# Norm scales taken out of the weights, packed mean squares and reordered instruction lists in a fused Mamba-2 and SwiGLU kernel

## The chip, the cores and the metric

The kernel runs on one core of one Trainium2 chip. The metric is device time of that core in microseconds (us), the median of several executions. Before the change it was 423.63 us (three runs, 423.05 to 426.83).

The engines that matter are TensorE (PE in the profile; PEld is its weight load), VectorE (DVE), ScalarE (ACT) and GpSimd (POOL). Each runs its own queue of instructions; semaphores order them against one another.

## The reference, cut to what matters

```python
# x: 4 x 8 heads x 768 x 32, chunks of 32 tokens; all float32
for c in range(nc):                      # Mamba-2 (SSD), chunk by chunk
    y_intra = einsum(M, xc)              # M = (C B^T) * causal decay
    y_inter = einsum(Cc, state) * exp(cum)
    y[chunk] = y_intra + y_inter
    state = exp(sum(la)) * state + sum(Bx)
x = y as (3072 tokens, 256)
rms = sqrt(mean(x * x) + 1e-6)           # then the feed-forward block
xn  = x / rms * rms_g
out = (silu(xn @ w_gate) * (xn @ w_val)) @ w_out     # d_ff = 1536
```

## The kernel before

The 3072 tokens go in six blocks of 512. For each block the kernel makes y from the chunks (its own chunks are of 128 tokens, 24 in all, taken in 12 pairs), norms it, and multiplies by the gate, value and output weights. From block 1 on the products are done in Strassen's way: seven products (`P.1` to `P.7`) for eight, with sums and differences of the inputs (`tx`) and of the weights (`sw`, `two`). The stage before block 1's first such product is called the prologue here. In it the float32 weights are also built out of the raw 64-bit words that they arrive in.

The last instruction of that building multiplies mantissa by power of two. It also carries the norm's gain, which differs between the two halves `t` of the model dimension, so it is done twice for every gate or value piece:

```python
def weight(k):
    ...
    if is_o:
        nc.vector.scalar_tensor_tensor(out=dst, in0=f, scalar=2.0 ** -20, in1=e, ...)
    else:
        for t in range(2):
            nc.vector.scalar_tensor_tensor(out=dst[:, t], in0=f[:, t],
                                           scalar=g20[:, t:t + 1], in1=e[:, t], ...)
```

The norm takes eight matmuls with one column of 1/256, then the roots on GpSimd and a transpose that spreads them:

```python
def norm_sums(blk):                               # step "ms"
    ps["m"] = ms = bank("ms", (P, NT))
    for k in range(NT):
        nc.tensor.matmul(out=ms[:, k:k + 1], lhsT=sqs[blk][:, k * P:(k + 1) * P],
                         rhs=mean1, start=True, stop=True)
def norm_roots():                                 # step "rs"
    nc.vector.tensor_scalar_add(me, ps.pop("m"), 1e-6)
    nc.gpsimd.tensor_tensor(out=rs, in0=me, in1=nhalf, op=ALU.pow)
```

(The loop has four steps; the trace shows eight instructions a norm, since a float32 matmul is two.) The y products of a pair of chunks go in this order, which one of the experiments changes:

```python
if not first:
    inter(0, True)        # state product of chunk 0: 32-row, 64-column tiles
intra(0, first)           # products inside the chunks: 32-column tiles
intra(1, False)
inter(1, False)           # state product of chunk 1
```

What runs when is set by lists of steps. There is one list for the prologue with block 0, one for block 1, one for blocks 2 to 4 and one for block 5. All engines' instructions are issued in the list's order. A few steps of the steady list:

```text
... hid.21.1 P.6.3 table C.12.0 Tt.1.1.0 ... s.1 A.0 S.0 Tt.1.0.1 y.0 take.6.2 ...
... s4.0 O.5.5 ms O.6.3 s2.5 s4.2 O.2.2 ... O.7.0 rs s4.1 O.7.1 ... rb O.7.3 ... xn ... tx
```

`P.k.j` is a Strassen product, `take` ScalarE's copy of it, `C`, `silu`, `hid` what follows it, `O` an output product, `A`, `S`, `y` the state and y products of a pair, `ex` an exponential, and `table` loads SiLU's activation table. `rb` spreads the roots and `xn` multiplies by them.

## Time and profile before

| | before |
|---|---|
| time, median | 423.63 us |
| span of the profiled run (itself timed 422.98) | 421.3 us |
| block 1's first Strassen product | 101.5 us |
| blocks 1, 2, 3, 4 (first product to next block's first) | 64.9, 65.0, 65.6, 65.5 us |
| block 5 to the last product's start, then the tail | 54.9, 3.8 us |
| table loads | 17 |

The page of the profile before, busy times with shares of the span and instruction counts, and the shares of the chain that ended last:

```profile
PE 410.1 (97%) x3094; PEld 347.5 (82%) x3094; DVE 309.1 (73%) x669; ACT 226.5 (54%) x455; POOL 38.0 (9%) x48
...
PE 80%; DVE 13%; ACT 5%; issue 1%; DVEq 0%
```

TensorE is busy for 97% of the span but carries only 80% of the chain. Another 18% lie on VectorE and ScalarE: about two thirds of it in the first 65 us, the rest in blocks 2 to 4, around 185, 225 to 235, 251 and 290 to 301 us. There something other than TensorE sets the pace, so there a change can win time without giving TensorE less to do. How much, these shares don't tell: TensorE is idle for only 3% of the span. The stages, the chain in order of time and the groups concerned are shown in the prediction.

### The profile page before, as it was taken

What the parts mean: (1) busy time and instruction counts of PE and PEld (TensorE: products, weight loads), DVE (VectorE), ACT (ScalarE), POOL (GpSimd) and SP (SyncE); (2) the same over time, 40 slices, a digit from 0 to 9 for tenths busy, and PEclk for the clock granted to TensorE, in tenths of its full rate; (3) what the DMA queues carried; (4) which work ended last, traced back from release to release, by engine and by line L of the source; (5) the groups of instructions that cost most, each with busy time, mean ns of one, the idle gap of its engine ahead of it and who ended that gap; (6) DMA issues with size and microseconds to landing.
All of it is one profiled execution on the core that took longest, in us unless ns stands there. A gap on an engine that the chain in (4) does not pass through costs nothing.

```text
span 421.3 us, 7884 instructions
## 1 busy us (share of the span) xinstructions
PE 410.1 (97%) x3094; PEld 347.5 (82%) x3094; DVE 309.1 (73%) x669; ACT 226.5 (54%) x455; POOL 38.0 (9%) x48
## 2 busy tenths in 40 slices
PE   7989999999999999999999999999999999999996
PEld 4575468888888899878899777899887899988896
DVE  5999999899748987467795676794766684546752
ACT  3989988569637454764324755333656331244510
POOL 2020001004000023000003200002200001000000
PEclk9999999999999999999999999999999999999999
DMA  9799479200133251003281003092100000100001
GB/s 117 212 205 283 157 250 138 65 0 8 44 68 83 52 101 44 8 4 97 64 131 26 33 0 101 9 160 35 51 1 2 2 2 1 51 0 2 0 2 50
DMA packets 86565, 27.99 MB, mean 66 GB/s; under 512 B 76001, under 2 KB 80353, under 8 KB 86529
## 3 DMA queue, kind: packets, MB, share of 16 engines
q1 hardware_dynamic: 82368, 27.24, 27.8%
q10 hardware_dynamic: 4160, 0.26, 0.8%
q8 instruction: 24, 0.39, 0.4%
q14 instruction: 13, 0.10, 0.1%
HBM read 24.22 MB, written 3.28 MB: 65 GB/s over the span
## 4 chain that ended last, share of the span: by engine, by line
PE 80%; DVE 13%; ACT 5%; issue 1%; DVEq 0%
PE gate L714 26%; PE o L794 20%; PE val L714 19%; PE o L746 5%; PE g L476 2%; DVE wgv L193 2%; PE y L558 2%; DVE m L181 2%; PE y L549 1%; PE tp L442 1%; DVE m L178 1%; ACT L L413 1%; PE ms L592 1%; DVE L L486 1%; DVE xn L615 1%
## 5 line engine op out<-in xcount | busy, mean ns | idle before, releaser
L726 DVE TENSOR_TENSOR c<-val,p 128x512 f32<-128x512 f32 x99 | 67.5, 687 | 40.6 <-PE val L714 24.8
L720 ACT COPY p<-gate 128x512 f32<-128x512 f32 x99 | 57.1, 588 | 73.6 <-PE gate L714 58.3
L714 PE MATMUL gate<-tx,sw 128*128 128x256 f32 x264 | 65.5, 382 | 1.1 <-ACT T L888 1.0
L714 PEld LDWEIGHTS gate<-tx,sw 128*128 128x128 f32 x264 | 49.3, 190 | 9.1 <-ACT T L888 1.7
L735 ACT ACTIVATE c<-c 128x256 f32<-128x256 f32 x99 | 39.1, 417 | 22.0 <-DVE c L726 21.9
L739 DVE TENSOR_TENSOR h<-c 128x256 f32<-128x256 f32 x99 | 39.4, 417 | 7.8 <-ACT c L735 7.8
L714 PE MATMUL val<-xn,sw 128*128 128x256 f32 x132 | 34.2, 382 | 0.0
L794 PE MATMUL o<-wo,h 128*128 128x128 f32 x240 | 33.8, 275 | 0.0
L714 PE MATMUL gate<-tx,wgv 128*128 128x256 f32 x132 | 33.8, 385 | 0.0
L714 PE MATMUL val<-xn,wgv 128*128 128x256 f32 x132 | 33.7, 380 | 0.0
L714 PE MATMUL val<-tx,sw 128*128 128x256 f32 x132 | 32.8, 380 | 0.0
L714 PE MATMUL gate<-xn,wgv 128*128 128x256 f32 x132 | 32.7, 380 | 0.0
L794 PE MATMUL o<-two,s 128*128 128x128 f32 x240 | 32.7, 276 | 0.0
L806 ACT COPY v<-o 128x256 f32<-128x256 f32 x15 | 5.6, 372 | 50.3 <-PE o L794 50.3
L794 PEld LDWEIGHTS o<-wo,h 128*128 128x128 f32 x240 | 30.9, 192 | 0.5
L794 PE MATMUL o<-two,h 128*128 128x128 f32 x240 | 30.9, 275 | 0.0
L794 PEld LDWEIGHTS o<-two,s 128*128 128x128 f32 x240 | 29.8, 192 | 0.2
L794 PEld LDWEIGHTS o<-two,h 128*128 128x128 f32 x240 | 28.8, 192 | 0.0
L577 POOL TENSOR_TENSOR sq<-sq 128x256 f32<-128x256 f32 x12 | 9.8, 813 | 207.4 <-ACT sq L576 178.1
L714 PEld LDWEIGHTS gate<-tx,wgv 128*128 128x128 f32 x132 | 24.3, 190 | 4.6 <-ACT p L720 1.0
L714 PEld LDWEIGHTS val<-tx,sw 128*128 128x128 f32 x132 | 25.0, 190 | 3.7 <-DVE two L757 0.3
L714 PEld LDWEIGHTS gate<-xn,wgv 128*128 128x128 f32 x132 | 24.6, 190 | 3.4 <-DVE c L726 0.3
(155 smaller groups left out, 705.0 us busy)
## 6 DMA issues: line engine op xcount, KB each, us to landing
L<-rowd SPq DMA_DIRECT2D x16, 512.0 KB, 4.4
xr<-in_x_dram SPq DMA_DIRECT2D x24, 128.0 KB, 3.3
wr<-in_moe_w_out_dram SPq DMA_DIRECT2D x6, 512.0 KB, 3.5
wr<-in_moe_w_gate_dram SPq DMA_DIRECT2D x5, 512.0 KB, 5.4
wr<-in_moe_w_val_dram SPq DMA_DIRECT2D x5, 512.0 KB, 5.9
out_dram<-ob SPq DMA_DIRECT2D x10, 256.0 KB, 2.1
br<-in_B_dram SPq DMA_DIRECT2D x22, 64.0 KB, 4.2
cr<-in_C_dram SPq DMA_DIRECT2D x22, 64.0 KB, 3.6
```

The costliest lines, as they stand in the source:

```text
L181: nc.vector.scalar_tensor_tensor(out=f, in0=lo.bitcast(U32), scalar=2.0 ** -32, in1=m, op0=ALU.mult, op1=ALU.add)
L193: nc.vector.scalar_tensor_tensor(out=dst[:, t], in0=f[:, t], scalar=g20[:, t:t + 1], in1=e[:, t], op0=ALU.mult, op1=ALU.mult)
L476: nc.tensor.matmul(out=g[:, 256 * i:256 * i + 256], lhsT=T[r, i, 0], rhs=T[r, i, 1:3].rearrange("p t m -> p (t m)"), start=(i == 0), stop= ...
L558: nc.tensor.matmul(out=y[o:o + 32, h // 4, i * P:(i + 1) * P], lhsT=s["x"][:, i, h], rhs=Ls[p][:, i, h], start=opens, stop=True, tile_posi ...
L577: nc.gpsimd.tensor_tensor(out=sqs[blk][:, tk], in0=sq2[:, 0], in1=sq2[:, 1], op=ALU.add)
L714: nc.tensor.matmul(out=dst[:, half[w]], lhsT=lhsT, rhs=rhs, start=(k in (1, 2, 5) and w == 0), stop=True, skip_group_check=True)
L720: nc.scalar.copy(out=t, in_=Xs[j])
L726: nc.vector.tensor_tensor(out=t, in0=Zs[j], in1=a, op=ALU.add)
L735: nc.scalar.activation(out=u, in_=src[:, half[0]], func=AF.Silu)
L739: nc.vector.tensor_tensor(out=hidden_tile(blk, j)[:, c // 10 - 1, c % 10 - 1], in0=u, in1=src[:, half[1]], op=ALU.mult)
L746: nc.tensor.matmul(out=o, lhsT=hs_[blk, f // 2][:, f % 2, k // 2, (k % 2) * P:(k % 2 + 1) * P], rhs=wo[:, f], start=opens, stop=(f == NF - ...
L794: nc.tensor.matmul(out=o[:, t * P:(t + 1) * P], lhsT=lhsT[:, t], rhs=rhs, start=(k in (1, 2, 4, 5) and j == 0 and t == 0), stop=True, skip ...
```

## The change

The intent: VectorE paces the prologue, so take the gain out of the weights (one multiply for a piece) and put it into y for block 0 and into the norm's multiply for the others. Make the mean squares with column-tiled matmuls (four tiles at once, then turned by a transpose). Aim at one SiLU table load per block. Write all four lists anew.

```diff
-        else:
-            for t in range(2):
-                nc.vector.scalar_tensor_tensor(out=dst[:, t], in0=f[:, t],
-                                               scalar=g20[:, t:t + 1], in1=e[:, t], ...)
+        nc.vector.scalar_tensor_tensor(out=dst, in0=f, scalar=2.0 ** -20, in1=e, ...)
...                                                  # block 0's y, on VectorE
+        for t in range(2):
+            nc.vector.tensor_scalar(out=yts[0][:, t, tk], in0=ps["y", p][:, t, 0:256],
+                                    scalar1=gcol[:, t:t + 1], scalar2=None, op0=ALU.mult)
...                                                  # ms, then mc, mt
-            nc.tensor.matmul(out=ms[:, k:k + 1], lhsT=sqs[blk][:, k * P:(k + 1) * P],
-                             rhs=mean1, start=True, stop=True)
+            nc.tensor.matmul(out=ms[32 * k:32 * k + 32, 0], lhsT=mean32,
+                             rhs=sqs[blk][:, k * P:(k + 1) * P], start=True, stop=True,
+                             tile_position=(0, 32 * k), skip_group_check=True)
+    def norm_out(blk):                               # step "mc", on ScalarE
+        nc.scalar.copy(out=mr, in_=ps["m", blk][:, 0])
+    def norm_back(blk):                              # step "mt"
+        nc.tensor.transpose(out=ps["m", blk][:, 1], in_=ps.pop(("mr", blk)), identity=ident)
...                                                  # norm, blocks 1 to 5
+            for t in range(2):
+                nc.vector.scalar_tensor_tensor(out=xns[blk][:, t], in0=yts[blk][:, t],
+                                               scalar=gcol[:, t:t + 1], in1=rb, ...)
...                                                  # steady list, a few steps
-  hid.21.1 P.6.3 table C.12.0 ... A.0 S.0 Tt.1.0.1 y.0 ... O.5.5 ms ... rs
+  P.1.2 P.3.1 hid.22.0 A.0 ... y.0 ... s2.2 ms ... mc O.5.4 ... mt ... rs ... O.3.0 Oadd.21 table O.3.1
```

The output weights' combinations (`two`) are now made in three parts for two, and some working tiles have other buffers: four of `e`, shared with the copies `p`. The lists are cut here; every one of the four is new.

## The prediction

> **What bounds the kernel now.** I first read the busy shares of the page, then the busy time of each engine by stage. TensorE first, in eight stretches cut where one 512-token block's products end and the next begin (the columns are from:to, length, busy time, instructions, granted clock, DMA share, GB/s):
>
> ```profile
> 18.00:64.00 46.00, 43.68 (x390) 1.00 0.74 212
> ...
> 107.00:166.60 59.60, 59.60 (x473) 1.00 0.28 58
> 166.60:232.00 65.40, 64.78 (x515) 1.00 0.28 58
> 232.00:298.00 66.00, 64.90 (x508) 1.00 0.27 57
> ```
>
> The same stretches for VectorE:
>
> ```profile
> 18.00:64.00 46.00, 45.00 (x97) 1.00 0.74 212
> 64.00:107.00 43.00, 39.89 (x78) 1.00 0.32 58
> 107.00:166.60 59.60, 45.11 (x94) 1.00 0.28 58
> ```
>
> There are two regimes. From 107 us on TensorE is full and VectorE has a quarter to spare. From 18 to 64 us, while weights are made from their raw words, VectorE is at 45.00 of 46.00 us and paces. The chain that ended last, in order of time, says the same; it lies on VectorE nearly all the way to 65 us:
>
> ```profile
> 26.17 0.47 DVE row L326
> ...
> 29.36 0.88 DVE wgv L193 x2
> 30.24 0.35 DVE m L178
> 30.61 0.69 DVE m L181
> 31.31 1.13 DVE xn L615
> ```
>
> A busy TensorE is not a dense one, so I also took start-to-start times. A 256-column fp32 product goes every 0.216 us (x8 takes 1.73 us in the chain), a 128-column one every 0.112. Set against such figures for each shape, TensorE loses some 6 us between 20 and 64 us, nearly nothing from 64 to 103, and about 0.8, 1.4, 2.1 and 1.5 us in blocks 1 to 4. Block 5 is dense up to its tail: the last product starts at 417.5 us and 3.8 us of copying out follow. New lists of steps can thus win back 12 us at the very most, and part of that is the changes of tiling mode described below, which no list removes. In blocks 2 and 3 one loss is the activation table loaded in the middle of the block (chain again):
>
> ```profile
> 185.08 1.28 ACT L997
> ...
> 186.64 0.37 ACT T L888
> 187.01 0.04 issue
> 187.05 0.43 PE A_ps L509 x16
> ```
>
> SiLU's set is active already at that point, so the load buys nothing, and the A products begin 0.78 us later than their predecessors allow. The other is the start of blocks 3 and 4, where a tx product waits for ScalarE (some 0.7 us, at 235.34 and 300.98).
>
> **What the Trainium skill says.** "TensorE: Matmul & The Clock Gate", Part 3, has matmuls on different column tiles run concurrently, and its LDWEIGHTS section has the load's time follow the columns alone. The trace agrees: a 128-column fp32 load takes 192 ns, one of 32 columns 109, and 32 column-tiled y matmuls of 128 columns go in 1.01 us, 0.032 us each. "TensorEngine Tiling (Array Packing)", Key Properties, says that changing the tiling mode drains TensorE; here the first full product after a packed run starts 0.2 to 0.3 us late. "VectorE: DVE Perf Modes", errata section, has a fixed cost per instruction; a 256-wide scalar_tensor_tensor of 502 ns against 685 for a 512-wide one shows it. "ScalarE: Activation LUTs", What ACT_TABLE_LOAD costs, gives 1283 ns plus a drain of some 1380. The load is 1283 ns here, but the next instruction starts 1.30 us after the load did (185.08 to 186.38): no such drain shows.
>
> **The change, part by part.** The groups that it touches:
>
> ```profile
> L193 DVE SCALAR_TENSOR_TENSOR wgv<-m,g,e 128x256 f32<-128x256 f32 x20 | 9.2, 502 | 0.2
> ...
> L592 PEld LDWEIGHTS ms<-mean,sq 128*128 128x128 f32 x48 | 6.1, 192 | 0.2
> L592 PE MATMUL ms<-mean,sq 128*128 128x1 f32 x48 | 5.9, 240 | 0.0
> ...
> L997 ACT ACT_TABLE_LOAD x3 | 3.8, 1283 | 0.1
> ...
> L189 DVE SCALAR_TENSOR_TENSOR wo<-m,e 128x512 f32<-128x512 f32 x6 | 4.1, 685 | 0.1
> ```
>
> *Norm scales.* The gate and value weights no longer carry the norm's gain, so each piece needs one instruction for two. Start to start, a large pair takes 0.80 us (29.36 to 30.16) and the single 512-wide form 0.61 (64.74 to 65.35). Ten large pieces save 1.9 us; four small ones, 0.53 against an assumed 0.36, save 0.7; the scale of the gain itself 0.14. Against that block 0's y is taken with four 256-wide instructions for two 512-wide copies, about +0.2. Net 2.5 us of VectorE work in the stage where VectorE paces. TensorE is near full there as well, so I count 2.2. Later blocks' norm multiplies in two halves for one instruction, +0.15 us each, beside output products: nothing.
>
> *Mean squares.* Eight instructions at 0.112 us (their weight loads set the pace, not the one column) become eight column-tiled ones, 8 x 0.032 = 0.25 us, with a change of mode, some 0.15, and one transpose, 0.11. That saves 0.4 us of TensorE a norm. Block 0's norm falls in the VectorE stage; the other five give 2.0. The chain of the norm grows by a ScalarE copy, a transpose and their waits, some 1.2 us, but the new lists place the sums early among output products of 0.45 us a step.
>
> *Table loads.* Counting the sets each list needs, I do not find one load a block. In blocks 2 and 3 the explicit load moves between the third and fourth exponential: exp, SiLU, exp, then SiLU again at the next block's first silu, four loads for three. Block 1 has two for three, and the total goes from 17 to 18. What matters is the place: the pair of loads now stands where ScalarE waits for output products. Walking those last steps with the trace's durations (four exponentials at 0.95, loads 1.28, copies 0.37 to 0.59), the fourth exponential ends about when the next block's first product does. So the 0.78 us before A goes, twice: 1.6 us.
>
> *Lists.* The tx differences now follow the norm's multiply at once; before, sub, scale and two additions, some 3 us, lay between them. That should remove the 0.7 us at two block starts, 1.4 us. But a block still opens with 12 copies in a row on ScalarE, and my walk of the new order finds the product that follows pair 0's last copy waiting some 0.6 us for it; in block 1, two weight combinations in front of a total cost TensorE perhaps 1 us. I count -1 for these new waits. In the prologue, block 0's three Strassen pairs start before y.2, and their products fill TensorE gaps: I allow 0.5. The output weights' combinations in three parts instead of two add about 0.8 us of VectorE work in block 1, where there is slack.
>
> The sum: 2.2 + 2.0 + 1.6 + 1.4 - 1.0 + 0.5 = 6.7 us, from 423.6 to about 416.9.
>
> **Rivals.** First, ScalarE becomes the bound at block borders: each extra load or late output copy delays the bank that the next products need. For it: 12 copies and a load in some 6 us. Against it: ScalarE is busy 31 of 65 us in a block. It would take back 1 to 1.5 us in each of blocks 1 to 4, leaving 419 to 421. Second, the prologue gives nothing, because TensorE (43.68 of 46.00) takes VectorE's place at once: then 418.5. Third, the lists pack everything: most of the 6 us lost from 20 to 64 and of the 5.8 in the blocks vanish; then 409 to 411. The table above allows it, but the old lists were packed too and left these.
>
> **Range and chances.** The terms are each uncertain by about half, and two of the rivals point up, one down: 411 to 421.5. Faster by over 2% needs 415.2 or less, 1.7 us below my centre with a spread of some 4: 0.35. Slower needs new stalls of some 16 us: 0.02.
>
> **What would show it.** Right: the gate and value weight group x14 instead of 28; the stage where VectorE is full some 2 us shorter; mean-square instructions on 128 x 32 tiles with some 0.5 us with the transpose; no load between silus before A in blocks 2 and 3 and no wait of A for T; 18 loads; blocks 2 and 3 near 63.5 us for 65.5 to 66; block 5 still some 58.6. Wrong: waits of gate products for the p copies at block starts adding up to over 2 us; multiply by the norm later than the last output product; or a VectorE stage as long as before.

## The result, and the profile after

The changed kernel took 418.38 us (median of four runs, 417.72 to 418.49); the kernel before, on the same chip, 423.68. The ratio of the fast runs is 0.9863, 95% interval 0.9818 to 0.9908: 1.4% faster, which is "within 2%". The ratios here are those on record, taken over all fast runs, so they are not quite the ratios of the medians that I quote. All runs below are of the fast state; their starts still differ, which the last section takes up; where it matters I give the difference of the quickest runs as well.

The page after:

```profile
PE 412.1 (99%) x3100; PEld 345.1 (83%) x3100; DVE 304.3 (73%) x665; ACT 229.7 (55%) x462; POOL 39.0 (9%) x48
...
PE 99%; DVE 0%; issue 0%
```

TensorE now carries the whole chain. The same stretches as in the prediction, cut at the new borders of the blocks, first TensorE and then VectorE (columns from:to, length, busy time, instructions, granted clock, DMA share, GB/s):

```profile
18.00:64.00 46.00, 46.00 (x428) 1.00 0.77 178
...
164.60:229.00 64.40, 64.40 (x516) 1.00 0.34 66
```

```profile
18.00:64.00 46.00, 44.62 (x94) 1.00 0.77 178
```

In the stage where weights are made, TensorE does 428 instructions in the 46 us for 390 before, and has no idle time in this view. VectorE is hardly less busy there (44.62 us for 45.00), so its busy time alone would not tell that it stopped pacing. The chain in order of time tells it. Where it lay on VectorE's weight instructions before, from 26 us on, it now goes from one group of TensorE products to the next; in block 2, y products follow gate products directly, where a table load stood before:

```profile
27.46 1.73 PE gate L658 x8
...
185.13 1.73 PE gate L732 x8
186.86 1.01 PE y L550 x32
```

The groups that the change touches, after (busy us, mean ns of one):

```profile
L186 DVE SCALAR_TENSOR_TENSOR wgv<-m,e 128x512 f32<-128x512 f32 (+1 forms) x14 | 8.4, 609 | 0.2 <-ACT e L170 0.2
...
L591 PE MATMUL ms<-sq,mean 128*32 128x128 f32 x48 | 2.7, 285 | 0.0
...
L600 PE MATMUL ms<-ident,mr 128*128 128x128 f32 x6 | 1.7, 282 | 0.0
```

There are 14 gate and value multiplies instead of 28 (two shapes, so 609 ns is a mixed mean), and the means are on 128 x 32 tiles with six transposes. All table loads together are 18, for 17, each still 1283 ns.

By stage, in us, with what the terms of the prediction come to in each (its sum laid out by place: the scales, one norm and the fill in the prologue; the counted -1.0 put in block 1; 0.78 and 0.7 where the prediction saw these waits; 0.4 a norm):

| stage | before | after | gain | predicted gain |
|---|---|---|---|---|
| to block 1's first Strassen product | 101.51 | 99.43 | 2.08 | 3.1 |
| block 1 | 64.90 | 65.16 | -0.26 | -0.6 |
| block 2 | 65.03 | 64.41 | 0.63 | 1.2 |
| block 3 | 65.64 | 64.34 | 1.30 | 1.9 |
| block 4 | 65.47 | 64.67 | 0.80 | 1.1 |
| block 5 to the last product's start | 54.91 | 54.91 | 0.00 | 0 |
| sum | | | 4.55 | 6.7 |

The profile of before happened to be one of its quicker starts (422.98 us) and the one of after not (418.49 us), so the two profiles show 4.5 us where the medians show 5.3.

### The profile page after: what moved, and what is told of

Same layout as the page of the kernel before. It is cut to its first block, busy times and chain, and to the rows that moved or that the text cites. A ratio compares the mean times of both kernels' runs of the same rounds, so it can differ in the third digit from the quotient of the medians.

```text
span 416.8 us, 7930 instructions
## 1 busy us (share of the span) xinstructions
PE 412.1 (99%) x3100; PEld 345.1 (83%) x3100; DVE 304.3 (73%) x665; ACT 229.7 (55%) x462; POOL 39.0 (9%) x48
## 4 chain that ended last, share of the span: by engine, by line
PE 99%; DVE 0%; issue 0%
PE gate L732 28%; PE o L815 23%; PE val L732 21%; PE o L764 5%; PE g L468 4%; PE gate L648 3%; PE y L550 3%; PE tp L434 2%; PE y L541 2%; PE gate L658 2%; PE e L363 1%; PE A_ps L501 1%; PE e L374 1%; PE rb L613 1%; PE idle L266 1%; PE ms L591 1%
## 5 line engine op out<-in xcount | busy, mean ns | idle before, releaser
L757 DVE TENSOR_TENSOR h<-c 128x256 f32<-128x256 f32 x99 | 41.1, 433 | 19.0 <-ACT c L753 18.9
L753 ACT ACTIVATE c<-c 128x256 f32<-128x256 f32 x99 | 38.2, 413 | 11.6 <-DVE c L744 10.7
L732 PE MATMUL val<-tx,sw 128*128 128x256 f32 x132 | 33.9, 384 | 0.0
L815 PEld LDWEIGHTS o<-wo,h 128*128 128x128 f32 x240 | 29.9, 192 | 1.0 <-issue 0.6
L732 PEld LDWEIGHTS val<-xn,sw 128*128 128x128 f32 x132 | 24.4, 190 | 4.2 <-issue 0.7
```

The costliest lines, as they stand in the source:

```text
L732: nc.tensor.matmul(out=dst[:, half[w]], lhsT=lhsT, rhs=rhs, start=(k in (1, 2, 5) and w == 0), stop=True, skip_group_check=True)
L753: nc.scalar.activation(out=u, in_=src[:, half[0]], func=AF.Silu)
L757: nc.vector.tensor_tensor(out=hidden_tile(blk, j)[:, c // 10 - 1, c % 10 - 1], in0=u, in1=src[:, half[1]], op=ALU.mult)
L815: nc.tensor.matmul(out=o[:, t * P:(t + 1) * P], lhsT=lhsT[:, t], rhs=rhs, start=(k in (1, 2, 4, 5) and j == 0 and t == 0), stop=True, skip ...
```

## The experiments

The theory after reading the two traces: the gain is the scales (in the prologue), the wait of A behind the table load and the waits at block starts (both through the lists), and less of the means than predicted. The rival: the new lists alone carry the gain, and the new operations are worth little or nothing. All twelve kernels gave right results. The kernel before had medians of 423.49 to 423.70 us in these calls; the kernels e8 to e11 ran on two other chips than the rest, and the quickest runs of the kernel before agree within 0.06 us on all three.

### Repetition

No edit: the changed kernel again.

> The changed kernel unaltered, as the anchor for the three others on the same chip. Expected: 418.4 us, 5.3 under before (ratio 0.987), within 0.4 us of the four runs on record; the profile again with no stall of TensorE over 0.4 us after 20 us.

It took 418.39 us (six runs, 418.23 to 418.47), ratio 0.9868 (0.9836 to 0.9899). The result stands, and the comparisons below use this value.

### All new operations in the old lists

```diff
 # the changed kernel's operations, the old four lists; only the new steps put in
- ms.0 wt.3 ... sums.2.0 rs ...          # prologue
+ ms.0 mc.0 wt.3 ... sums.2.0 mt.0 rs.0 ...
- s4.0 O.5.5 ms O.6.3 ... O.7.0 rs s4.1  # steady list
+ s4.0 O.5.5 ms mc O.6.3 ... O.7.0 mt rs s4.1
```

> All the new operations in the old lists of steps (the copy and the turn of the mean squares put right after the sums and right before the roots, the three thirds of the output weights' combinations where the two halves were). Theory 1 (removed work counts wherever TensorE is full): 2.0 us from the mean squares plus about 1.3 from VectorE work in the prologue: 420.3. Rival (the lists give nearly all, the operations nothing without them): 423 or more. If the longer norm chain is not hidden in the old lists, a wait of the roots shows and the time stays over 422.

It took 423.01 us (22 runs), ratio 0.9993 (0.9968 to 1.0017): no gain that stands out of the noise (0.5 us by medians, 0.6 by quickest runs). At first sight this is the rival's result, but the trace shows why. ScalarE in the prologue (start, duration; in brackets the idle time just before and who ended it):

```profile
25.56 0.27 ACT L597 COPY mr<-ms 128x128 f32<-128x128 f32 x1 [1.62 <-PE ms L591]
25.72 0.75 ACT L167 ACTIVATE e<-wr,kinks 128x512 int16<-128x512 int16 x1
```

The copy of the sums, put right after them in the list, reached the head of ScalarE's queue before they were done. ScalarE stood for 1.62 us with the weight pieces' powers behind it, although those needed nothing from TensorE. What comes of it on VectorE, some 6 us later:

```profile
31.56 1.22 DVE L629 TENSOR_TENSOR xn<-yt,rb 128x1024 f32<-128x1024 f32 x1 [0.78 <-ACT r L618]
```

The roots' copy `r` was late, VectorE waited for it in the stage where it paces, and TensorE then waited for VectorE and ScalarE (0.93 us at 32.84, 0.55 at 35.45, from the start-to-start times). In blocks 2 to 4 it was the other new step (waits, summed over these blocks: total, times, longest):

```profile
PEld rb L613 <- POOL rs L607: 1.2, 3, 0.4
```

The transpose stood directly before the roots' addition, so the chain of the norm was longer by it and TensorE waited 0.4 us a block for GpSimd: more than the packed sums save (blocks 2 to 4 are 0.18 us longer each than before). The Trainium skill has ScalarE's queue as strictly in order ("TensorE: Matmul & The Clock Gate", the specification table at its top, engine queue depth); the 1.62 us, with work behind that was ready, agree with it.

### Old scales, old means, and both, in the new lists

```diff
 # e2: the gain back in the weights (and, not shown, the old copies of y and norm multiply)
-        nc.vector.scalar_tensor_tensor(out=dst, in0=f, scalar=2.0 ** -20, in1=e, ...)
+        for t in range(2):
+            nc.vector.scalar_tensor_tensor(out=dst[:, t], in0=f[:, t],
+                                           scalar=g20[:, t:t + 1], in1=e[:, t], ...)
 # e3: the one-column matmuls back; mc and mt do nothing
+            nc.tensor.matmul(out=ms[:, k:k + 1], lhsT=sqs[blk][:, k * P:(k + 1) * P],
+                             rhs=mean1, start=True, stop=True)
 # e4: both
```

> The changed kernel with the first part alone undone: gains in the gate and value weights again (28 multiplies in place of 14), y of block 0 copied, norm applied in one multiply. Prediction's step (VectorE paces the prologue, so its 2.5 us count nearly whole): 418.4 + 2.2 = 420.6. Rival (TensorE is so near full in the prologue that VectorE's saving is slack): 418.4 to 419.0.

> The changed kernel with the mean squares alone undone (eight one-column products a norm, no copy and no turn). Theory (TensorE is full on the whole chain, so its work counts one for one): six norms x 0.34 us = +2.0: 420.4. Rival (the norm lies beside waits that end elsewhere): 418.4 to 418.8. If the extra latency of the copy and the turn had cost something in the changed kernel, the step up is smaller than 1.5.

> The new lists of steps (and the buffers that go with them) with both the scales and the mean squares undone. If the parts add: 418.4 + what e2 and e3 cost, by the prediction 422.8; by the rival in which the scales are slack, 420.5. If the lists had been made for the new operations and do harm with the old ones: over 423.7.

They took 420.24, 419.35 and 421.54 us (ratios to before 0.9916, 0.9892, 0.9926). Against 418.39 the scales are worth 1.85 us in the new lists, the means 0.96, and both 3.15, near their sum of 2.81. By the quickest runs (417.72 of the changed kernel, 420.12, 419.07 and 421.00 of these) it is 2.4, 1.35 and 3.3. The medians mix executions with an early and a late start of TensorE's full clock (last section). Of traces with the same start, those with one part undone span 418.1 and 417.2 us, against 416.1 of the changed kernel without its table loads (below; its blocks are as long as the changed kernel's); with both undone it is 419.4 against 416.8 of the changed kernel's own profile, both with a late start. That makes 2.0 for the scales, 1.1 for the means and 2.6 for both. The new lists by themselves, with the buffers and the three parts, are worth 423.6 - 421.5 = 2.1 us.

The means came to half of what I had counted. TensorE around the sums of block 2, first with the old means in the new lists and then in the changed kernel:

```profile
211.78 0.61 PE L813 MATMUL o<-wo,h 128*128 128x128 f32 x4
212.22 0.95 PE L591 MATMUL ms<-mean,sq 128*128 128x1 f32 x8
213.03 0.69 PE L813 MATMUL o<-wo,h 128*128 128x128 f32 x4
213.56 0.61 PE L813 MATMUL o<-two,h 128*128 128x128 f32 x4
```

```profile
211.82 0.61 PE L815 MATMUL o<-wo,h 128*128 128x128 f32 x4
212.36 0.42 PE L591 MATMUL ms<-sq,mean 128*32 128x128 f32 x8
212.72 0.71 PE L815 MATMUL o<-wo,h 128*128 128x128 f32 x4
213.27 0.61 PE L815 MATMUL o<-two,h 128*128 128x128 f32 x4
...
215.95 0.27 PE L600 MATMUL ms<-ident,mr 128*128 128x128 f32 x1
216.06 0.61 PE L815 MATMUL o<-two,s 128*128 128x128 f32 x4
```

Read the starts. The four output products before the sums take 0.44 us to the next start with the old means (211.78 to 212.22) but 0.54 with the packed ones, and those after them 0.53 and 0.55 where a free-running group needs 0.45. From 211.8 to the second group after, the old form needs 1.78 us and the new one 1.45, and the transpose adds 0.11 (215.95 to 216.06): 0.22 us saved, not 0.4. In the single starts the change to 32-column tiles costs about 0.1 us on the product before, 0.2 from the last packed one to the next product, and 0.1 on that product's successor. So the change of mode costs 0.4 us, part of it on neighbours that do not bear its name, where I had counted 0.15. The lengths of three blocks agree: old means minus new is 0.23, 0.23, 0.05 and 0.23 us in blocks 1 to 4. In block 3 of the changed kernel GpSimd's addition of the second half of the squares ended only at 276.66 us, after the sums had begun (276.52); their second half started at 276.72, and the sums took 0.18 us longer than in the other three.

### One table load fewer, before and after

```diff
 # e5: the kernel before without the explicit load (lists of block 1 and of blocks 2 to 4)
- ... hid.21.1 P.6.3 table C.12.0 ...
+ ... hid.21.1 P.6.3 C.12.0 ...
 # e6: the changed kernel without it
- ... O.3.0 Oadd.21 table O.3.1 ...
+ ... O.3.0 Oadd.21 O.3.1 ...
```

> The kernel before with the explicit SiLU load taken out of blocks 1 to 3. The prediction's step (the load in mid-block delays A by 0.78 us in blocks 2 and 3): 423.7 - 1.6 = 422.1, and no wait of A for T. Rival (another wait takes its place, for instance the copies of the next products): 423.0 to 423.7. Loads: 14 by my count, 17 before, because block 1's return to exp goes too.

> The changed kernel with the explicit SiLU load taken out of blocks 1 to 3. The prediction's step (the two extra loads at block ends hide beside output products): no change, 418.0 to 418.6. Rival (ScalarE is late at the border, the loads cost 1.28 us each there): 415 to 417. Loads: 18 before the edit, 13 after it by my count.

Without the explicit loads, the kernel before took 422.18 us (ratio 0.9941, 0.9915 to 0.9967): 1.5 us less by medians (1.4 by quickest runs), for the predicted 1.6. The trace has it where the load stood before A: blocks 2 and 3 are 0.68 and 0.69 us shorter, blocks 1 and 4 as long as before. All its loads are 13, for 17 before and 14 expected. Of the changed kernel, the same edit takes five of its 18 loads away (6.4 us of ScalarE), and it took 418.10 us, 0.3 less than the repetition; the quickest runs, 417.86 us and 417.72, have the other sign. So the place of the load before A is worth 1.4 to 1.5 us, the number of loads elsewhere nothing, and ScalarE does not bind at the borders of the changed kernel's blocks.

### The new scales in the old lists

```diff
 # e9: the first experiment's kernel with the old means; its lists are the old ones,
 # the new weights, y and norm multiplies, three-part "two" and buffers stay
```

> The old lists and the old mean squares with the new scales alone (and the three-part combinations). If VectorE's saving of 2.5 us counts by itself in the old prologue, as the prediction had it: 423.7 - 1.9 = 421.8. If the old order makes TensorE wait at other results instead, as the waits in e1's prologue suggest: 423.0 to 423.7.

It took 419.98 us (nine runs), ratio 0.9925 (0.9893 to 0.9957): 3.5 us less than before. Both theories missed it. The whole gain lies ahead of block 1: its first Strassen product starts at 97.97 us for 101.51, earlier than in the changed kernel (99.43). Set against the run of all new operations, the new means in the old lists cost 3.0 us (2.7 by the quickest runs) instead of saving anything. This kernel differs from the one before in more than the scales, though: the buffers and the three-part combinations are in it too.

### The sums earlier in the old lists

```diff
 # e10: the first experiment's kernel; ms mc mt rs some ten output steps earlier in blocks 1 to 4
- O.1.2 O.1.3 silu.22.5 ... O.5.5 ms mc O.6.3 ... O.7.0 mt rs
+ O.1.2 O.1.3 ms mc silu.22.5 ... O.1.4 O.5.2 mt s2.0 O.1.5 rs ... O.5.5 O.6.3
```

> e1 with one thing moved: in blocks 1 to 4 the sums, their copy, their turn and the roots stand some ten output steps earlier. If the wait of the norm's transposes for the roots (0.37 us in each of blocks 2 to 4) is what ate the mean squares' saving of 0.23 us a norm in the old lists: 423.0 - 1.1 = 421.9, and no wait of the transposes for GpSimd. Rival (the saving is lost in any case): 423.0.

It took 424.62 us (22 runs), ratio 1.0032 (1.0008 to 1.0055): worse by 1.6 us than the kernel that it was to mend (1.4 by the quickest runs), and again outside both expectations. Blocks 2 to 4 are 0.47 us longer each. The reason is the copy again. Moved with the sums, it stood ahead of the last silu operations in ScalarE's queue:

```profile
217.39 0.27 ACT L597 COPY mr<-ms 128x128 f32<-128x128 f32 x1 [3.10 <-PE ms L591]
```

The hidden values were late, and two groups of output products started 0.32 and 0.34 us late (at 218.79 and 220.25 us in the trace, both waiting for VectorE's hidden values). In the first experiment's kernel the copy stood 3.10 us too in this block (at 220.03), but with nothing behind it that was ready, and no product was late for it. Giving the chain of the norm more time did not help while the copy moved along with the sums.

### The copy moved away from the sums

```diff
 # e11: the first experiment's kernel
- ms.0 mc.0 wt.3 row.1 parts.1 yt.1 pow.4 ydone.1      # prologue, block 0's norm
+ ms.0 wt.3 row.1 parts.1 yt.1 pow.4 mc.0 ydone.1
- Otake.1 O.4.1 O.2.1 ... O.5.5 ms mc O.6.3 s2.5 s4.2 O.2.2 O.6.4 ... O.7.0 mt rs   # blocks 2 to 4
+ Otake.1 O.4.1 ms O.2.1 ... O.5.5 mc O.6.3 s2.5 s4.2 O.2.2 mt O.6.4 rs ... O.7.0
 # block 1's norm in the prologue ("ms.1 mc.1") and block 1's list are left as they were
```

> Kernel: all new operations in the old lists (as e1, 423.0 us), with the steps of the mean squares moved so that ScalarE never stands at the copy of the sums with other work behind it: block 0's copy comes after the powers of the combinations instead of right after its sums, and in blocks 1 to 4 the sums go some five output steps earlier while the copy, the transposes and the roots stay late. Theory (ScalarE and its strict order: the copy stood at the head of ScalarE's queue and held 1.6 us of other work in the prologue, and in blocks 2 to 4 the transposes waited 0.36 us for GpSimd's roots): the saving of the new means comes back, so the new scales' 420.0 less 6 x 0.23 = 418.6 us, between 418 and 419.5; the combination of Q in the prologue no longer waits for r, and no weight load of the second transposes waits for GpSimd. Rival (the new means can't pay in the old lists wherever the copy stands, for the tiling-mode changes and the extra instructions cost what they save): 420 to 423 us. As in every run here, starts with a late clock grant (3.4 us longer) are set apart when the runs are compared.

It took 419.93 us (11 runs, 419.71 to 423.83), ratio 0.9929 (0.9896 to 0.9962). That is 3.1 us less than the first experiment's kernel, 2.7 by the quickest runs of each, and nothing but steps of the norm was moved: the order in the queues was the cause. Yet it is 1.3 us above the theory's number and no better than the old means in the same lists (419.98), as the rival has it. The trace tells which part held. Blocks 2 to 4 take 64.80, 65.42 and 65.26 us for 65.03, 65.65 and 65.48 with the old means, so the packed means do save 0.2 us a block in old lists too. Against the first experiment's kernel these blocks are 0.4 us shorter each, 1.2 in all; the rest of the gain lies in the prologue. The edit did less than its recorded expectation says, though: I had left the copy beside its sums at block 1's norm in the prologue, and something was lost there:

```profile
64.69 0.27 ACT L597 COPY mr<-ms 128x128 f32<-128x128 f32 x1 [1.52 <-PE ms L591]
64.85 0.76 ACT L167 ACTIVATE e<-wr,kinks 128x512 int16<-128x512 int16 x1
...
67.54 1.06 ACT L738 COPY p<-gate 128x512 f32<-128x512 f32 x2
```

ScalarE stood 1.52 us again. The next copies of Strassen products started at 67.54 us; with the old means in the same lists they are at 65.48, in a trace that is 0.27 us ahead. TensorE waited 0.55 us for them (at 68.66), and lost 0.8 us in all between 60 and 99 us; block 1 lost another 0.3, which I did not trace to one wait. In this execution, itself timed 420.41 and so 0.5 us over the median, these losses, 1.1 us, outweigh the 0.7 us of blocks 2 to 4; by the medians gain and loss cancel. That the losses would go with the last two copies moved is argued and not shown.

### Fewer changes of tiling mode

```diff
 # e7: the changed kernel, y products in another order
-        if not first:
-            inter(0, True)
-        intra(0, first)
+        intra(0, True)
         intra(1, False)
+        if not first:
+            inter(0, False)
         inter(1, False)
 # e8: e7, without the table load, and in four places (blocks 1 to 4) A and S moved to stand right ahead of y
- P.3.1 hid.22.0 A.0 turn.1.1 ... L.0 take.6.2 S.0 P.2.3 ... hid.22.1 y.0 C.11.2
+ P.3.1 hid.22.0 turn.1.1 ... L.0 take.6.2 P.2.3 ... hid.22.1 A.0 S.0 y.0 C.11.2
```

> The changed kernel with the products for y in another order: both chunks' inner products first, then both products with the state, so that a pair changes the tiling mode once less. Theory (TensorE is full, and a change of mode costs 0.19 us plus 0.13 for the second instruction of a run): eight of the twelve pairs have a state at their first chunk, 8 x 0.32 = 2.6 us: 415.8. Rival (the change of mode is hidden by other work, or the state's products now wait): 418 or more.

> The version meant to beat both: the changed kernel with the y order of e7, without the explicit SiLU loads of e6, and with the A products put directly before y where the lists had them apart (first pair of blocks 2 to 4, second pair of block 1), since both use 32-column tiles. If changes of tiling mode are what TensorE still loses: e7 416.5, -0.3 for the loads, -0.25 for each of four places: 415.2. Rival (A now waits for its bank or y for the state): 416.5 or more.

They took 416.48 and 415.99 us, ratios 0.9803 and 0.9809 (0.9778 to 0.984). The y products of block 1's first pair (made in the prologue), in the changed kernel and in the reordered one:

```profile
54.01 0.45 PE L541 MATMUL y<-T,S 32*64 32x128 f32 x8
54.39 1.08 PE L550 MATMUL y<-L,xr 128*32 128x128 f32 x32
55.40 0.45 PE L541 MATMUL y<-T,S 32*64 32x128 f32 x8
55.78 0.43 PE L501 MATMUL A_ps<-xr,Bd 128*32 128x64 f32 x16
```

```profile
53.19 1.08 PE L550 MATMUL y<-L,xr 128*32 128x128 f32 x32
54.20 0.67 PE L541 MATMUL y<-T,S 32*64 32x128 f32 x16
54.80 0.43 PE L501 MATMUL A_ps<-xr,Bd 128*32 128x64 f32 x16
```

From the first y product to A it takes 1.77 us in one and 1.61 in the other: with the two state products together there is one change of tiling mode fewer, worth 0.16 us. Eight of the twelve pairs of chunks have both state products (each of the four sequences starts with none), which makes 1.3 us; the quickest runs differ by 417.72 - 416.30 = 1.4, the medians by 1.9. Blocks 1 to 4 are 0.32, 0.30, 0.16 and 0.46 us shorter, where their pairs (two, one, one and two) give 0.32, 0.16, 0.16 and 0.32. The theory on record, 0.32 us a pair, was twice too high. Moving A next to y (and taking the load out, worth nothing) brings some 0.5 us more, for 1.0 expected of A; block 3 got 0.28 us shorter by it, but block 2 0.10 longer, so what A's place is worth is not settled. The last kernel beats both, the changed one by 2.4 us; its fast runs are 1.9% below those of before, and the interval leaves open whether it is over 2%.

## Why the prediction was right

The predicted time was 416.9 us with a range of 411 to 421.5; it is 418.38. "Within 2%" had the highest chance and is what came. That VectorE's saved work would count nearly whole in the prologue, and where the gains would lie, was as predicted; that TensorE would then carry the whole chain was only in the rivals. The total is no lucky sum: 2.0 for the scales, 1.1 for the means and 2.1 for the lists with the load's new place (counted 2.2, 2.0 and 2.5) make 5.2 of the 5.3 us measured. Inside the lists' term, though, a cost set too high offsets gains set too high. The terms of the sum of 6.7 us, one by one:

**Norm scales, 2.2 us: right in size.** The multiplies went from 28 to 14, and putting the two-instruction form back costs 1.85 us (2.4 by the quickest runs, 2.0 by traces of like start). The stage up to block 1 is shorter by 2.08 us for 3.1 predicted with one norm and the fill. The late start that fell into the profile of after accounts for 0.6 us of the difference: without its table loads the changed kernel has the same prologue, and in a trace with an early start it reaches block 1 at 98.80 us, 2.7 earlier than the kernel before. What I had not expected: the scales with the new buffers and three-part combinations, in the old lists, shorten this stage by 3.5 us, more than the whole change does there. Which of these parts makes the surplus was not tried, so it stays open.

**Mean squares, 2.0 us: mis-sized by half.** The mechanism is right. Packed and turned, one norm saves 0.22 us and not 0.4. The mis-sized term is "with a change of mode, some 0.15": it measured 0.4 us, 0.1 ahead, 0.2 at the end and 0.1 on the successor, while the packed matmuls went a little faster than counted. Five norms (block 0's was not counted) at 0.22 are 1.1 us, and the kernel without the packed means lies 0.96 (medians), 1.1 (traces of like start) or 1.35 us (quickest runs) higher. I had the 0.2 to 0.3 us after a packed run from the trace of before, wrote it down, and then put in a smaller figure.

**Table loads, 1.6 us: right.** Removing the load from the kernel before gives 1.5 us (0.69 a block for 0.78), the total went from 17 to 18 as counted, and the loads where they now stand cost nothing.

**Lists, 1.4 - 1.0 + 0.5 us.** The waits at the starts of blocks 3 and 4 are gone, as predicted: after 64 us no late start of over 0.4 us is left on TensorE. Of the new waits, counted with 1.0 us, block 1 had its part: with some 0.2 us saved on its norm it still got 0.26 longer, so about 0.5 was added (with only the lists changed it is 0.44 longer). In the later blocks none showed, so this term was too large by about half. The gains of blocks 2 and 3, 0.63 and 1.30 us for 1.2 and 1.9, are nevertheless short; their lengths are 64.4 and 64.3 us and not "near 63.5". The means account for 0.17 us of it in block 2 and 0.35 in block 3, the wait before A for 0.09 in each. A now stands apart from y there: from start to start this costs 0.15 us after the last A product, 0.06 after the next one and 0.09 more before y, less 0.04 for the direct step from A to y, some 0.25 us. That is about all that is missing, but the run that puts A next to y again doesn't confirm its size (it has block 2 longer).

**The 12 us "at the very most".** Too high, as the remark beside it feared. Between 20 and 64 us, the late starts of over 0.3 us in the trace of before sum to some 3.7 us (1.2 at 23.31 and 1.15 at 57.04 among them). I put the rest of the 6 us down mostly to changes of tiling mode, without a run that shows it. No list of the same steps removes those, though another order of the products inside one step does, as the y products show.

**The rivals.** The first, ScalarE as the bound at block borders, fell when taking the loads out changed nothing. The second, a prologue that gives nothing, fell with the 2.08 us and with the run of the old scales. Its time, 418.5 us, lies next to the measured 418.38 by chance; it doesn't even follow from its own terms, since 416.9 with the scales and the fill lost is 419.6. (Likewise 1 to 1.5 us in each of four blocks would have put the first rival at 421 to 423, not 419 to 421.) The third was right in that TensorE is now 99% of the chain, and wrong in what that is worth, for the reason just given.

**Two readings to put right.** The 502 ns against 685 compare a scalar taken from memory with one in the instruction; with the latter, the 256-wide form takes 418 ns in the changed kernel, so the fixed part of an instruction is some 0.15 us by these two (an estimate) and not 0.3. And the table load at 185.08 us renews a set that is active; real switches are in the last section.

**Not foreseen.** The prediction reckoned operations and lists as separate terms. They are not: the new operations in the old lists gave 0.1%, because a copy put in right after its sums stopped ScalarE and a transpose put in right before the roots made TensorE wait. In the lists of the change, the copy `mc` comes some steps after `ms`, and in blocks 1 to 4 the transpose well before the roots. In the prologue, where ScalarE's other work stands behind, neither copy waits there (26.32 and 73.44 us), and the packed means pay.

## What to carry to other kernels

A new step in an in-order queue costs what it makes wait behind it, not what it takes itself: put the reader of a result into the list where the result is ready, and look in its engine's timeline for an idle time right before it, and for work behind it that was ready (without such work 3.10 us of idle time cost nothing here). Before counting what a packed matmul saves, measure the change of mode from start to start with the neighbours on both sides, and keep products of one mode together. Try an operation and the list made for it both together and apart, since here one run alone gave not even the sign of what the packed means are worth.

## What the Trainium skill lacked or had wrong

- "TensorEngine Tiling (Array Packing)", Key Properties, says that a change of tiling mode drains TensorE and gives no figure for it. Here a norm's change to 32-column tiles and back cost 0.4 us in all: 0.1 on the product before, 0.2 after the last packed one, 0.1 on the next. One change fewer in the y products was worth 0.16 us a pair.
- "ScalarE: Activation LUTs", What ACT_TABLE_LOAD costs, adds a drain of some 1380 ns to the load of 1283 at every switch to a different set. The load takes 1283 ns here, and at switches between SiLU and the exponential (before, at 94.20, 96.57 and 98.30 us) it began 0.02 us after the last activation's end and the next one started 1.30 us after it did: no such drain shows.
- "TensorE: Matmul & The Clock Gate", Part 1, has the full clock come around 4 us into sustained matmul activity, give or take 0.5. The first matmul starts at 1.11 us here, and in some executions the full clock came much later than that, although TensorE is shown busy from 2 to 8 us without a break. In the profile of before, a 128-column transpose takes 0.27 us from 6.45 us on; in that of after, 0.42 us up to 8.62 and 0.27 from 10.76; in that of the sums moved earlier in the old lists, still 0.42 us at 15.79 (from start to start 0.21 us for 0.11). The column of the granted clock reads 1.00 in all these stretches; the clock records in the packed traces begin only at 5.05, 10.11 and 16.82 us, which agrees with the durations. The kernel before took about 423.0, 423.6 or 426.6 us, the last in 7 of 27, 9 of 23, 5 of 30 and 3 of 16 runs. A late start adds about 0.6 us in the profiles (block 1 at 99.43 us for 98.80 with the same prologue), a very late one went with 427.77 us for a quickest run of 423.77. The middle group has a second cause: in the profile of the kernel before without its loads (422.23 us for a quickest of 421.65) the clock records read one half from 58.45 to 61.87 us, in mid-run, and 256-column products took 634 ns for 379.
- The same part has nothing on how a kernel's order of instructions bears on such late starts. Here none of the 48 runs of the seven kernels with the new lists was in the late group, but 45 of the 175 with the old ones were (24 of 96 of the kernel before, 21 of 79 of the others). So something in the new lists avoids the very late start. The medians hardly show this part of their gain (in the call of the repetition the means of all runs differ by 5.8 us, the medians by 5.1). Which steps do it was not tried.
- No page has a figure for an instruction held at the head of ScalarE's queue. The specification table of "TensorE: Matmul & The Clock Gate" names the strict order; here it was 1.62 and 1.52 us of idle time in two places. Moving the first of these copies, with the steps of blocks 2 to 4, won 3.1 us (2.7 by quickest runs), of which 1.2 lie in those blocks.
